# Four fill steps moved from the first expert unit into attention, and one difference moved to GpSimd

## The chip, the cores and the metric

One core of one Trainium2 chip runs the program. The core's engines are TensorE (PE, with its weight loads PEld), VectorE (DVE), ScalarE (ACT), GpSimd (POOL) and SyncE (SP), which issues most DMAs. The metric is the device time of one execution in microseconds.

## The reference

Attention with four sink tokens and a window of 128, then a mixture of eight experts whose gate is normalised by eight Sinkhorn rounds over all tokens:

```python
q, k, v: (4, 8, 768, 64)                      # batch, heads, sequence, head_dim
keep = is_sink | in_window
scores = np.where(keep, scale * q @ k.T, -1e9)
a = softmax(scores);  x = (a @ v) laid out as (3072, 512)

P = np.exp(x @ w_gate - max)                  # (3072, 8)
for _ in range(8):
    P /= P.sum(1, keepdims=True) + 1e-09
    P /= P.sum(0, keepdims=True) + 1e-09
    P *= N / E
for e in range(8):
    out += P[:, e:e + 1] * (np.maximum(x @ w1[e], 0.0) @ w2[e])   # w1: 512x1024, w2: 1024x512
```

## The kernel before

All matrices are kept as a rounded high part and a low part, and a product is three matmuls (high-high, high-low, low-high). The token rows are worked in three parts of 1024.

**Attention.** 48 units, numbered n = 12 b + 2 i + hh over the four sequences b, the six query blocks i of 128 rows and the two halves hh of the heads. The loop `for n in range(-2, L + 3)` runs one round for each: in round n PE does the scores of unit n+1 (L468, into the PSUM banks st0 to st3), the values of unit n-1 (L527), the query and key transposes of unit n+2 (L433), and the transposes of unit n's probabilities (L489, into st1 and st2). Around them VectorE adds the mask (L471), ScalarE exponentiates (L474), GpSimd scales (L478), ScalarE casts the transposed keys and queries (L437) and both split the transposes into PT (L350, cast on ScalarE, subtraction on VectorE). The first block of a sequence (i = 0) has no previous block and no sinks: half the probability transposes and half the value matmuls. PE's order is the program's (`manual_schedule(engines={PE})`); the order on the other engines in this stage is a planner's.

**Fill.** The generator `plain()` computes expert 0 for the first part in 128 steps, numbered 0 to 127: a step is six 128x256 matmuls of a first product (`plain_g1`, L606; two steps make one sum, after which ScalarE does the ReLU, L611, and VectorE its low part, L612), or three 128x512 matmuls of a second product (`plain_g2`, L622). Both kinds alternate, but for the first eight steps (g1 alone) and the last eight (g2 alone). Its weights are split into W1 and W2f by L350; W2f has two buffers. The steps are taken by `run_fill` in the attention rounds from round 5 on, one after the first half of the values and one at the end of the round (92 in all), by the 28 `tick` steps behind attention (REST), and by the eight slots `S_` of the first expert unit (n = 0), which has no earlier unit's second product to put there.

**REST.** In these 28 steps all engines follow the program's order. Step by step they also run the Sinkhorn rounds (`sinkhorn_step`: L48 to L59, with one small matmul, L56, that needs VectorE's csum, L53) and make the x-forms T1, T3 and T2: `make_form` subtracts two raw blocks in two halves (L973), and `form_steps` splits the result (L817 on ScalarE, L818 on VectorE). T1 is made in step 7 and T3 in step 12 on GpSimd, T2 in step 18 on VectorE; `sums1(1)` on GpSimd (L689 to L692) follows in step 23. T2 is split in steps 21 and 22.

**Expert units.** From here each unit of 256 hidden columns runs seven products (M1 to M7, six matmuls each, L791) and the previous unit's second product in the slots `S_`:

```python
STEPS = ["M2", "M1", "M5", S_, "M3", S_, "M6", S_, S_, "M7", S_, S_, "M4", S_, S_]
```

M1, M6, M7 and M4 share PSUM bank c1: each of them waits until VectorE has added the bank's last content into C (L1006, followed by ReLU L1001 and low part L1002). M2, M5 and M3 share c2, copied by ScalarE (L998). The unit's weights W1f come in four pieces, split in unit n for unit n+1 by L817 and L818. Second products (L1035) are added up by VectorE (L630 for fill, L1042 for units).

Parts two and three of the tokens run the same units with stored weights (L791 on W1q, L1350 on W2q).

Of the kernel before, what the change touches and what calls it, by code (L numbers as in the profile page):

```python
# [229 lines left out]
def tile_sink_attention_moe(ctx: ExitStack, tc: tile.TileContext, q, k, v, wg, w1, w2, out):  # L230

    nc = tc.nc
# [75 lines left out]
    def split_gate():  # L308
        for kc in range(KC):
            nc.vector.tensor_copy(wgr[:, kc, :], zero)  # L310
        nc.vector.tensor_copy(wgr[:, :, 0:E], wg_raw)
        nc.vector.tensor_sub(wgr[:, :, E:2 * E], wg_raw, f32(wgr[:, :, 0:E]))
        nc.vector.tensor_add(sel, ident[0:2 * E, 0:E], ident[0:2 * E, E:2 * E])
# [82 lines left out]
    units = [(b, i, hh) for b in range(B) for i in range(NB) for hh in range(2)]  # L396
# [5 lines left out]
    def load_sinks(b):  # L402
        vs = seq[b] = att.tile([SK, D], F32, name="vs")
        for r0 in range(0, SK, NK):
            (nc.sync if b else nc.scalar).dma_start(vs[r0:r0 + NK, :], v[b, :, 0:SINK, :])
# [10 lines left out]
    def load_block(b, i):  # L416
        raws[b, i] = r = [att.tile([P, H, D], F32, name=nm) for nm in ("kr", "qr", "vr")]
        cuts = (0, HH, H) if (b, i) == (0, 0) else (0, H)
        for ts in (((r[0], k), (r[1], q)), ((r[2], v),)):
            for h0, h1 in zip(cuts, cuts[1:]):  # L420
                for t, src in ts:
                    nc.sync.dma_start(t[:, h0:h1, :], src[b, h0:h1, i * P:(i + 1) * P, :].rearrange("h p d -> p h d"))
# [88 lines left out]
    def values(n, pr):  # L511

        b, i, hh = units[n]
        u = us[n]
        if pr == 0:
            u["O"] = ps_o.tile([P, NP, 2, P], F32, name="O")
        cs = slice(pr * P, (pr + 1) * P)
        ops = []
        ws = (1,) if i == 0 else (0, 1)
        for j, w in enumerate(ws):  # L520
            V = us[n - 2 + 2 * w]["V"]
            for x_, y_ in ((0, 0), (0, 1), (1, 0)):
                ops.append((V[:, x_, cs], u["PT", pr][:, y_, j]))
        if i:
            ops.append((seq[b][:, hh * HH * D:][:, cs], u["PS"].unsqueeze(1).broadcast_to([SK, 2, P])))
        for j, (x_, y_) in enumerate(ops):
            nc.tensor.matmul(u["O"][:, pr], lhsT=x_, rhs=y_, start=(j == 0), stop=(j == len(ops) - 1))  # L527
        if pr == NP - 1:
            store_x(n)
# [51 lines left out]
    def gate_step():  # L581
        if gates and next(gates[0], 0) == 0:
            gates.pop(0)
            gate_step()
# [48 lines left out]
    def plain():  # L633

        second = iter(())
        flip = 0
        for us_ in ((0, 1), (2, 3)):
            W = {u: load_plain(0, u) for u in us_}
            for g in range(NG):
                for th in range(2):  # L640
                    hs = []
                    flip = 1 - flip
                    for u in us_:
                        h = hpr.tile([P, 2, HT], F32R, name=f"h{flip}{u % 2}").rearrange("p w (c t) -> p w c t", c=2)
                        for c in range(2):
                            for _ in plain_g1(W, u, c, h, g, th):
                                yield
                                if next(second, 0) is None:
                                    yield
                        hs.append(h)  # L650
                    for _ in second:
                        yield
                    second = plain_g2(W, hs, us_, g, th)
        for _ in second:
            yield

    fill = plain()
# [3 lines left out]
    def run_fill(k_):  # L661
        for _ in range(k_):
            next(fill, None)
# [15 lines left out]
    def blocks(r1):  # L679
        A = r1.rearrange("p (a k) (b f) -> p a b k f", k=KH, b=2)  # L680
        return A[:, 0, 0], A[:, 1, 0], A[:, 0, 1], A[:, 1, 1]

    def sums1(n):

        A11, A12, A21, A22 = blocks(R1[n])
        if n not in ST:
            ST[n] = new_sums()
        S = ST[n]
        nc.gpsimd.tensor_add(S[:, 3], A21, A22)  # L689
        nc.gpsimd.tensor_sub(S[:, 0], S[:, 3], A11)  # L690
        nc.gpsimd.tensor_sub(S[:, 2], A11, A21)
        nc.gpsimd.tensor_sub(S[:, 1], A12, S[:, 0])  # L692
# [25 lines left out]
    with tc.manual_schedule(engines={PE}):  # L718
        for n in range(-2, L + 3):
            on = lambda j: 0 <= j < L  # L720
            if on(n + 2):
                b, i, hh = units[n + 2]
                if hh == 0:
                    with (tc.high_priority() if n == -2 else nullcontext()):
                        load_block(b, i)
                    if i == 0:
                        load_sinks(b)
            if n == -2:
                nc.sync.dma_start(wg_raw, wg.rearrange("(k p) e -> p k e", p=P))
            if n == 2:  # L730
                with tc.issue_after(us[1]["split"][1]):
                    split_gate()
            gates += later
            later.clear()
            if on(n + 1):
                scores(n + 1, 0)
                scores(n + 1, 1)
            if on(n - 1):
                values(n - 1, 0)
            if n >= START:  # L740
                run_fill(1)
            gate_step()
            for j in (0, 1) if n == -2 else (n + 2,) if n >= 0 else ():
                if on(j):
                    transpose_qk(j)
            if on(n):
                transpose_p(n, 0)
                with (tc.issue_after(us[n - 1]["scaled"]) if n > 1 else nullcontext()):
                    split_v(n)
            gate_step()  # L750
            if on(n):
                transpose_p(n, 1)
            if on(n - 1):
                values(n - 1, 1)
            gate_step()
            if on(n) and units[n][1]:
                transpose_sinks(n)
            if on(n) and units[n][1:] == (0, 1):
                with tc.issue_after(us[n]["scaled"]):
                    split_sinks(units[n][0])  # L760
            if n >= START:
                run_fill(1)
            first_w1(n)
        while gates:
            gate_step()
# [203 lines left out]
    def make_form(form, eng=nc.vector):  # L969

        a, b = {"T1": ("B12", "B11"), "T3": ("B22", "B12"), "T2": ("B22", "B11"), "T4": ("B21", "B22")}[form]
        for c in HALVES:
            eng.tensor_sub(raw[PLACE[form]][:, :, c], raw[a][:, :, c], raw[b][:, :, c])  # L973
# [188 lines left out]
    for k in (0, 2, 4, 6, 10, 12, 13, 17, 19, 20, 24, 26, 27):  # L1162
        todo[k].append(sinkhorn_step)
    for k, f in ((7, lambda: make_form("T1", nc.gpsimd)), (12, lambda: make_form("T3", nc.gpsimd)),
                 (18, lambda: make_form("T2")), (23, lambda: sums1(1))):
        todo[k].append(f)
    form_steps(todo, {"T1": (14, 15), "T2": (21, 22), "T3": (24, 25)})
    for k in range(REST):
# [6 lines left out]
    for n in range(len(units0)):  # L1175
        todo = plan(n)
        if n == len(units0) - 1:
            assert not list(side)
            load_x(1, (1, 0), (0, 0), (0, 1), (1, 1))
        run, then, hs[n] = first(n)  # L1180
        sec = second(n - 1, hs[n - 1]) if n else None
        bank = "o" if n else "held1"
        sk_psum = lambda shape, bank=bank: ps0.tile(shape, F32, name=bank, bufs=2 if bank == "o" else 1)
        tight = n == len(units0) - 1
        for k, m in enumerate(STEPS):

            early = m in ("M1", "M6", "M7") and (n < 2 or tight) or m == "M4" and tight
            if early:
                run(m)
                rest = then[m]()  # L1190
                if m == "M4":
                    rest()()
            for f in due.pop(clock[0], ()):
                f()
            for f in todo[k]:
                f()
            if m != S_:
                if not early:
                    run(m)
                    rest = then[m]()  # L1200
                if rest and not (early and m == "M4"):
                    line = due.setdefault(clock[0] + 1, [])
                    line.insert(1 if early else len(line), rest())
            elif n:
                next(sec)()
            else:

                next(fill)
            clock[0] += 1
    assert next(fill, 0) == 0  # L1210
    for k in (16, 17):
# [314 lines left out]
```

## Time and profile before

| what | value |
|---|---|
| median of 3 runs | 2140.49 us (2140.0 to 2141.41) |
| profiled execution | 2140.46 us |
| its span, first to last instruction | 2138.7 us |
| busy: PE, DVE, ACT, POOL | 99%, 72%, 41%, 35% |
| mean granted TensorE clock | 0.997 |
| attention rounds with the changed lines (24, 25, 36, 37) start | 152.8, 158.1, 224.0, 229.2 us |
| REST and the first unit | about 302 to 322.6 us, 322.6 to 338.75 us |

How to read the rows: in the timeline a row has its start in us, its length, the engine, the line, the operation, the tiles out<-in, the shape and the count, and in brackets how long the engine stood idle before it and what ended that. Rows of one kind that follow each other are merged. A window row has the stretch, its length, the busy time of PE, PEld, DVE, ACT and POOL with their counts, the granted clock, the DMA share and GB/s. Matmuls are pipelined and their ends are modelled, so the distance from one row's start to the next is read, not the length.

### The profile page before, as it was taken

How to read it: one execution, taken by the hardware profiler on the slowest of the kernel's cores; microseconds unless marked ns; L12 is line 12 of the kernel's file. 1: busy time of each engine (PE TensorE's matmuls, PEld its weight loads, DVE VectorE, ACT ScalarE, POOL GpSimd, SP SyncE). 2: the span in 40 equal slices, each digit the busy share in tenths (PEclk: the TensorE clock that was granted, in tenths of full speed). 3: DMA queues.
4: the chain of work that ended last, by engine and by line, in shares of the span. 5: the costliest groups of instructions: out<-in, count | busy, mean ns of one | idle time of the engine just before them, and what ended most of it. 6: DMA issues, size and time to landing. Idle time of an engine off the chain costs nothing.

```text
span 2138.7 us, 31819 instructions
## 1 busy us (share of the span) xinstructions
PE 2120.3 (99%) x10501; PEld 1769.8 (83%) x10501; DVE 1538.8 (72%) x2821; ACT 881.9 (41%) x1867; POOL 750.4 (35%) x950
## 2 busy tenths in 40 slices
PE   8999999999999999999999999999999999999998
PEld 7898897888888888888888888888888888888887
DVE  8878868877777776766666666666657666666666
ACT  7777745444444444442333223332333223332322
POOL 7766643233232331232223222233323232233223
PEclk9999999999999999999999999999999999999999
DMA  7434326999999987686666666667866666666662
GB/s 184 95 84 101 86 80 230 314 307 312 294 309 293 310 290 251 216 282 205 204 192 201 208 192 205 203 200 262 297 204 196 199 207 194 200 207 189 205 197 85
DMA packets 397643, 453.83 MB, mean 212 GB/s; under 512 B 99680, under 2 KB 265760, under 8 KB 396576
## 3 DMA queue, kind: packets, MB, share of 16 engines
q1 hardware_dynamic: 397080, 451.57, 68.0%
q8 instruction: 86, 1.41, 0.3%
q14 instruction: 85, 0.70, 0.1%
q10 hardware_dynamic: 392, 0.16, 0.0%
HBM read 314.17 MB, written 137.46 MB: 211 GB/s over the span
## 4 chain that ended last, share of the span: by engine, by line
PE 94%; DVE 3%; ACT 1%; DMA 1%; issue 0%; POOL 0%; SPq 0%; ACTq 0%; DVEq 0%
PE c L791 40%; PE o L1350 20%; PE held L1350 8%; PE held L1035 7%; PE o L1035 7%; PE O L527 3%; PE st L468 2%; PE st L489 1%; PE o L622 1%; PE g L606 1%; ACT sc L474 1%; PE st L433 1%; DVE sc L471 0%; PE O L557 0%; PE st L606 0%
## 5 line engine op out<-in xcount | busy, mean ns | idle before, releaser
L817 ACT CAST hf<-w 128x512 fp32r<-128x512 f32 x448 | 265.0, 620 | 561.5 <-POOL w L1317 299.2
L1350 PE MATMUL o<-hf,W2q 128*128 128x512 f32 x1920 | 472.0, 389 | 0.0
L1350 PEld LDWEIGHTS o<-hf,W2q 128*128 128x128 f32 x1920 | 360.0, 188 | 75.5 <-DVE acc L1364 0.8
L791 PE MATMUL c<-T,W1q 128*128 128x512 f32 x1530 | 389.0, 389 | 0.2 <-DVE w L1298 0.2
L818 DVE TENSOR_TENSOR hf<-w,hf 128x512 fp32r<-128x512 f32 x448 | 330.4, 766 | 74.3 <-ACT hf L817 66.8
L791 PEld LDWEIGHTS c<-T,W1q 128*128 128x128 f32 x1530 | 286.7, 188 | 60.9 <-DVE w L1298 1.2
L1364 DVE TENSOR_TENSOR acc<-o,acc 128x512 f32<-128x512 f32 x298 | 204.6, 687 | 171.5 <-PE o L1350 171.5
L791 PE MATMUL c<-B,W1q 128*128 128x512 f32 x1134 | 278.3, 389 | 0.0
L1317 POOL TENSOR_TENSOR w<-w 128x512 f32<-128x512 f32 x64 | 82.7, 1292 | 493.2 <-DVE w L1299 486.6
L791 PEld LDWEIGHTS c<-B,W1q 128*128 128x128 f32 x1134 | 212.5, 188 | 44.0
L1298 DVE TENSOR_TENSOR w<-c,M 128x512 f32<-128x512 f32 x192 | 132.3, 689 | 138.8 <-PE c L791 133.1
L1294 ACT COPY M<-c 128x512 f32<-128x512 f32 x192 | 112.7, 587 | 250.4 <-PE c L791 250.3
L1350 PE MATMUL held<-hf,W2q 128*128 128x512 f32 x768 | 194.8, 389 | 0.0
L791 PE MATMUL c<-T,W1f 128*128 128x512 f32 x672 | 171.2, 390 | 0.2
L1035 PE MATMUL held<-W2f,h 128*128 128x512 f32 x672 | 171.1, 390 | 0.0
L1035 PE MATMUL o<-W2f,h 128*128 128x512 f32 x672 | 170.6, 389 | 0.1
L1350 PEld LDWEIGHTS held<-hf,W2q 128*128 128x128 f32 x768 | 144.0, 188 | 29.9
L1332 POOL TENSOR_TENSOR w<-w 128x512 f32<-128x512 f32 x64 | 105.7, 1651 | 176.2 <-DVE hf L818 176.2
L1035 PEld LDWEIGHTS o<-W2f,h 128*128 128x128 f32 x672 | 126.0, 188 | 27.0 <-DVE acc L1042 0.9
L791 PEld LDWEIGHTS c<-T,W1f 128*128 128x128 f32 x672 | 125.7, 188 | 27.1 <-ACT M L998 0.5
L1035 PEld LDWEIGHTS held<-W2f,h 128*128 128x128 f32 x672 | 125.8, 188 | 26.4 <-DVE W2f L818 0.5
L844 POOL TENSOR_TENSOR r<-r 128x256 f32<-128x256 f32 x27 | 20.1, 744 | 359.6 <-ACT M L998 210.0
(216 smaller groups left out, 3100.3 us busy)
## 6 DMA issues: line engine op xcount, KB each, us to landing
W2q<-w2s SPq DMA_DIRECT2D x448, 256.0 KB, 3.2
W1q<-w1s SPq DMA_DIRECT2D x444, 256.0 KB, 2.8
w1s<-W1f SPq DMA_DIRECT2D x56, 896.0 KB, 7.6
w2s<-WT SPq DMA_DIRECT2D x136, 256.0 KB, 3.4
r<-in_moe_w_dram SPq DMA_DIRECT2D x64, 512.0 KB, 4.0
w2s<-W2f SPq DMA_DIRECT2D x56, 256.0 KB, 4.8
PB<-psd SPq DMA_DIRECT2D x16, 512.0 KB, 4.2
w2s<-W2f SPq DMA_DIRECT2D x56, 128.0 KB, 6.5
```

Of the source, the lines that this page charges most:

```text
L468: nc.tensor.matmul(ps[h], lhsT=Q[r0:r0 + D, a, pr, :], rhs=K[r0:r0 + D, c, pr, :], start=(j == 0), stop=(j == 2))
L527: nc.tensor.matmul(u["O"][:, pr], lhsT=x_, rhs=y_, start=(j == 0), stop=(j == len(ops) - 1))
L791: nc.tensor.matmul(ps, lhsT=w1(a, k), rhs=x[:, b, k, :], start=(start and j == 0), stop=(stop and j == len(TERMS) - 1), skip_group_check=n ...
L817: nc.scalar.copy(dst[:, 0], src)
L818: at(1, lambda: nc.vector.tensor_sub(dst[:, 1], src, f32(dst[:, 0])))
L1035: nc.tensor.matmul(o, lhsT=h[c, th][:, a, off:off + P], rhs=W2F[n][:, w, c, :], start=(begin and c == 0 and j == 0), stop=(end and c == 1 ...
L1294: nc.scalar.copy(t, T["c2"])
L1298: nc.vector.tensor_add(w, T["c1"], T[m])
L1317: nc.gpsimd.tensor_sub(S3, T["A11"], T["A21"])
L1332: at(k, lambda: nc.gpsimd.tensor_sub(T["A11"], w, T["A11"]))
L1350: nc.tensor.matmul(o, lhsT=W2Q[part, n, m][:, a, k * P:(k + 1) * P], rhs=F[part, n, H_OF[m]][:, w, :], start=(j == 0 and (begin or not hol ...
L1364: nc.vector.tensor_add(sums[m, k], o, sums[m, k])
```

## The change

Three edits. In the rounds of the third and fourth sequences' first blocks (n = 24, 25, 36, 37) the fill call at the end of the round takes two steps instead of one. The fill then has four steps fewer left for the first expert unit: its last four `S_` slots (two behind M7, two behind M4) find none, for which `next` gets a default. And T2's subtraction in REST's step 18 is issued on GpSimd.

```diff
             if n >= START:
-                run_fill(1)
+                run_fill(2 if on(n) and units[n][0] > 1 and units[n][1] == 0 else 1)
             first_w1(n)
...
     for k, f in ((7, lambda: make_form("T1", nc.gpsimd)), (12, lambda: make_form("T3", nc.gpsimd)),
-                 (18, lambda: make_form("T2")), (23, lambda: sums1(1))):
+                 (18, lambda: make_form("T2", nc.gpsimd)), (23, lambda: sums1(1))):
...
-                next(fill)
+                next(fill, None)
```

## Prediction, made before the change was run

> **What bounds the kernel now.** I read the page first, then the stages by windows, then the chain of waits and the timeline of each engine around the four changed rounds and the first expert unit.
>
> ```profile
> span 2138.7 us, 31819 instructions
> PE 2120.3 (99%) x10501; PEld 1769.8 (83%) x10501; DVE 1538.8 (72%) x2821; ACT 881.9 (41%) x1867; POOL 750.4 (35%) x950
> ...
> 302.40:322.60 20.20, 19.83 (x128) 17.51 (x127) 16.24 (x41) 6.42 (x14) 9.19 (x8) 1.00 0.44 155
> ...
> 331.50:338.70 7.20, 7.12 (x31) 5.59 (x32) 6.91 (x15) 3.21 (x7) 0.70 (x2) 1.00 0.01 2
> 338.70:364.60 25.90, 25.52 (x109) 19.25 (x108) 24.96 (x45) 14.25 (x27) 6.25 (x8) 1.00 0.92 299
> ```
>
> TensorE carries nearly the whole span, so the same matmuls in another place change the time only by the waits they fill or leave open. The windows (stretch, its length, then busy time of PE, PEld, DVE, ACT, POOL, then the clock) show two kinds of stage. In the 28 steps between attention and the first unit (302.4 to 322.6) DVE has slack. From the middle of the first unit on (331.5 to 338.7) DVE is busy 6.91 of 7.20 us, and in the second unit 24.96 of 25.90: there PE and DVE are both full. What the change takes out of PE there is worth only what DVE allows.
>
> The chain of waits around rounds 24 to 26 (start, length, what):
>
> ```profile
> 154.84 0.73 PE g L606 x6
> ...
> 157.45 0.71 PE o L622 x3
> 158.16 0.60 PE st L468 x6
> ...
> 159.32 1.88 ACT sc L474 x7
> ...
> 163.76 0.43 DVE sc L471
> ...
> 168.44 1.22 PE st L468 x9
> ```
>
> A fill step of six 128x256 matmuls (L606) holds the chain for 0.73 us, one of three 128x512 (L622) for 0.71. Up to the scores at 158.16 the chain is PE; from there to the scores at 168.44 it runs through ScalarE, GpSimd and VectorE. So a step added at the end of round 24 (before 158.16) moves the chain by its length, and one at the end of round 25 can hide, as far as PE has slack there.
>
> **The change part by part.** *Added steps.* Each pair of changed rounds gets one L606 and one L622 step: 0.73 + 0.71 = 1.44 us of PE, twice. How much of it hides, from the timelines:
>
> ```profile
> 152.81 0.99 PE L468 MATMUL st<-KQ 64*128 64x260 f32 x12
> 153.59 0.43 DVE L471 CUSTOM_DVE_ANT_0 sc<-st,mask 128x260 f32<-128x260 f32 x1 [0.56 <-PE st L468]
> ...
> 162.75 1.24 PE L468 MATMUL st<-KQ 64*128 64x260 f32 x12
> ...
> 166.23 0.36 ACT L611 ACTIVATE h<-g 128x256 fp32r<-128x256 f32 x1
> 166.50 0.57 ACT L437 CAST KQ<-st 128x512 fp32r<-128x512 f32 x1
> ...
> 234.00 1.31 PE L468 MATMUL st<-KQ 64*128 64x260 f32 x12
> ...
> 235.10 0.43 DVE L471 CUSTOM_DVE_ANT_0 sc<-st,mask 128x260 f32<-128x260 f32 x1
> ```
>
> Where DVE waits for the scores, L471 starts 0.78 us after them (152.81 to 153.59). In round 26 PE starts its scores at 162.75 and would now start them at 162.75 + 1.44 = 164.19, so L471 starts at 164.97 where it started at 163.76: 1.21 us later, 0.23 hidden. From there the chain is not PE's. One thing shortens it: the second half of a g1 sum falls to the end of round 25 instead of round 26's first slot, so its ReLU (L611, 0.36) can run while ScalarE waits for scores and no longer stands before the cast L437; that would start 166.50 - 166.23 = 0.27 earlier. Third sequence: +1.21 - 0.27 = +0.94. Fourth sequence, in the same way: 234.00 + 1.44 + 0.78 = 236.22 against 235.10, +1.12; the ReLU of round 38 stays where it is, since that sum's second half still falls to the first slot. Both: +2.06 us. Bounds: +2.88 if nothing hides; and what follows in round 39, where the freed W2f buffer counts:
>
> ```profile
> 239.52 1.15 ACT L350 CAST W2f<-r 128x512 fp32r<-128x512 f32 x2
> ...
> 239.78 1.72 PE L468 MATMUL st<-KQ 64*128 64x260 f32 x11 [0.21 <-DVE PT L350]
> ...
> 240.24 1.56 DVE L350 TENSOR_TENSOR W2f<-r,W2f 128x512 fp32r<-128x512 f32 x2
> ```
>
> These two splits wait for the last fill step that reads the old W2f (step 67 of 0 to 127), which was in round 38 and is now in round 37, and DVE does them ahead of the next L471. Moved into cover they give back 1.56 us; moved into the bare chain of round 38, while the other unit's pair takes their old place in round 39, they cost 1.56 more. The order of these engines is a planner's, and no row shows which; I take 0, and both ends for the range. The casts of W1 move a round in the same manner, with the same two signs.
>
> *T2's difference on GpSimd.*
>
> ```profile
> 309.21 2.75 POOL L973 TENSOR_TENSOR x<-x,x 128x512 f32<-128x512 f32 x2 [0.23 <-DMA x<-xscr]
> 311.92 0.90 POOL L689 TENSOR_TENSOR ST<-r 128x256 f32<-128x256 f32 x1
> ...
> 315.26 1.82 DVE L973 TENSOR_TENSOR x<-x,x 128x512 f32<-128x512 f32 x2
> ...
> 318.22 0.86 PE L622 MATMUL O<-W2f,h 128*128 128x512 f32 x3
> 319.45 0.39 PE L56 MATMUL st<-csum,ones 128*128 128x8 f32 x2 [0.37 <-DVE csum L53]
> ```
>
> DVE loses two subtractions, 1.82 us. GpSimd gains two of about 2.75 / 2 = 1.38 each, right behind T3's (it has no step to wait for), and would be done at 311.96 + 2.75 = 314.7, ahead of DVE's 317.1. Queued behind them on GpSimd stands only the next unit's sums1 (from 311.92), whose product is first used in unit 0's step 13 (W1f's third piece, behind the 337.90 of a row below): covered by over 15 us. DVE is late exactly here: PE waits at 319.45 for csum, which it would otherwise pass at 318.22 + 0.71 = 318.93. That 0.52 us goes. Bounds: 0 and -0.52 (PE has no second wait there). The page "SBUF — State Buffer" of the Trainium skill, section "SBUF: two separate sides", speaks against the move: GpSimd and a DVE instruction with two SBUF inputs lock one another out for the whole instruction. The trace bears this out in one place:
>
> ```profile
> 231.60 1.27 POOL L414 TENSOR_TENSOR VS<-vm,VS 32x512 fp32r<-32x512 f32 x1
> ...
> 231.61 1.28 DVE L475 TENSOR_SCALAR st<-st 128x2 f32<-128x2 f32 x1
> ```
>
> The tiny L475 started with L414 and ended with it. If each T2 half held DVE so, DVE would lose 2 x 1.38 = 2.76 and save 1.82: by the rule the sum is 0.52 to 0.52 + 0.94 worse. I take the gain, because DVE's own T2 already stood beside GpSimd's sums1 and took 1.82.
>
> *Four steps fewer in unit 0.* Its eight slots now hold the steps only up to M6; the two slots behind M7 and the two behind M4 are empty.
>
> ```profile
> 331.46 1.63 PE L622 MATMUL o<-W2f,h 128*128 128x512 f32 x6
> 332.92 1.54 PE L791 MATMUL c<-T,W1f 128*128 128x512 f32 x6
> 334.31 1.52 PE L622 MATMUL o<-W2f,h 128*128 128x512 f32 x6
> 335.13 0.63 DVE L1006 TENSOR_TENSOR C<-c,M 128x512 f32<-128x512 f32 x1
> 335.91 1.63 PE L791 MATMUL c<-T,W1f 128*128 128x512 f32 x6
> 337.37 1.53 PE L622 MATMUL o<-W2f,h 128*128 128x512 f32 x6
> 337.90 1.02 DVE L818 TENSOR_TENSOR W1f<-r,W1f 128x512 fp32r<-128x512 f32 x2
> 338.75 2.88 PE L791 MATMUL c<-B,W1f 128*128 128x512 f32 x12
> ...
> 341.73 0.69 DVE L1006 TENSOR_TENSOR C<-c,M 128x512 f32<-128x512 f32 x1 [0.41 <-PE c L791]
> ```
>
> The fills there took 335.91 - 334.31 = 1.60 and 338.75 - 337.37 = 1.38, 2.98 us in all, of which 0.2 was already waiting. But M4 (335.91) writes bank c1 and must wait for DVE's L1006 (335.13 to 335.76), which stands in DVE's fixed order behind work that does not get shorter; it starts where it does now. And the next unit's M2 (338.75) needs the first W1f piece, whose DVE half runs from 337.90 and takes about 0.69 (two in 1.02, the second half as large): it can start at 338.62. So 2.98 us of PE work turns into waits and only 338.75 - 338.62 = 0.13 comes back. Ends: -0.13 and -2.98. I take -0.13, because DVE's 6.91 of 7.20 us is in the same order before and after; only one accumulate (L630) leaves, behind this point. `next(fill, None)` costs nothing: it issues no instruction.
>
> **Sum:** +2.06 - 0.52 - 0.13 = +1.41 us. The profiled execution took 2140.46 us (its span and 1.8 around it), 0.03 under the median of 2140.49, so both give 2141.9.
>
> **The rivals.** *Unit 0 gives all back* (DVE's order turns out to follow PE): 2141.9 - 2.85 = 2139.0. Against it speaks the 6.91 of 7.20; for it, the 0.41 us that DVE waits for PE at 341.73, right behind.
>
> *The W2f splits fall into cover*: 2141.9 - 1.56 = 2140.3. *They fall before round 38's scores, and the other pair into round 39*: 2143.5. For the second speaks that the buffer gets free in round 37, just ahead of the round with least PE work.
>
> *The lock keeps T2's gain*: 2142.4 to 2143.4.
>
> *Slower: the clock.* Behind M7 and M4 PE would idle some 1.6 and 1.2 us within 6 us. Early in the span the clock fell in such a place:
>
> ```profile
> 16.00:20.00 4.00, 2.74 (x17) 2.38 (x16) 3.81 (x11) 3.87 (x12) 3.82 (x7) 1.00 1.09 361
> ...
> 20.00:28.00 8.00, 6.96 (x41) 6.02 (x42) 7.84 (x28) 5.58 (x17) 5.75 (x15) 0.57 0.46 95
> ...
> 19.62 1.31 PE L468 MATMUL st<-KQ 64*128 64x260 f32 x12 [1.26 <-DVE KQ L438]
> ```
>
> PE was busy 2.74 of 4 us with one wait of 1.26, and over the 8 us behind it the mean granted clock was 0.57. If the same comes here, PE loses 8 x (1 - 0.57) = 3.4 us (an estimate from this row) in a stage without slack: 2145.3. It decides from a loss of 2.9 us on (2144.8). The Trainium skill, "TensorE: Matmul & The Clock Gate", section "Why this matters for your kernels", allows gaps up to about 3 us; by that rule the clock holds and the sum stays as it is. The 1.26 us wait above says that shorter ones can do it.
>
> **How the numbers follow.** Forecast 0.47 (own range 2140.6 to 2143.0), unit 0 gives back 0.10, W2f in cover 0.12, W2f in the chain 0.13, lock 0.08, clock 0.10. No change means within 0.2%, 4.3 us (2136.2 to 2144.8), about what a measurement of this kernel can tell. Slower: half of the clock case and the tail of W2f in the chain, 0.10. Faster needs several gains at once: 0.03. The range 2138.4 to 2145.0 leaves out about half the clock case and some of the first rival's tail.
>
> **What would show it.** Right: rounds 26 and 38 start their scores about 1.2 us later against round 24's and 36's than now; no wait of L56 for csum in the 28 steps; PE idle behind M7 and M4 with L1006 and L818 as releasers; M6 of unit 0 to the next M2 still about 7.2 us. Wrong: that last distance near 4.4 us, a round 39 that is 1.5 us shorter or a longer round 38, or a granted clock under 1.00 behind 330 us.

## The result and the profile after

| | before | after |
|---|---|---|
| median (14 runs each) | 2140.47 us (2139.64 to 2141.41) | 2145.27 us (2144.31 to 2146.41) |
| ratio, with its 95% interval | 1 | 1.0023 (1.0014 to 1.0031) |
| profiled execution | 2140.46 us | 2145.48 us |

The change made the kernel 4.8 us slower; the forecast was +1.4, and 2145.27 lies just above the range, which ended at 2145.0. The page of the kernel after has nearly the same work in a longer span:

```profile
span 2143.7 us, 31817 instructions
PE 2119.1 (99%) x10501; PEld 1769.7 (83%) x10501; DVE 1538.2 (72%) x2819; ACT 882.4 (41%) x1867; POOL 756.1 (35%) x952
```

To see where it went, both spans are cut at the same PE instructions, the first scores (L468) of a round or the first matmul of a product. The table has the length before and the difference after:

| stretch | before, us | after |
|---|---|---|
| start to round 12 | 81.41 | +0.30 |
| rounds 12 to 23 | 71.41 | +0.01 |
| rounds 24 to 35 (third sequence) | 71.15 | -0.08 |
| rounds 36 to 40 (fourth sequence) | 29.87 | **+5.49** |
| rounds 41 to 45, then up to the 28 steps | 48.55 | -0.30 |
| the 28 steps | 20.20 | -0.48 |
| unit 0, M2 to M5 | 2.87 | +1.14 |
| unit 0, M5 to M7 | 7.46 | +0.03 |
| M7 to the next unit's M5 | 8.68 | -0.39 |
| the rest | 1797.14 | -0.78 |

The last row is not the change's work: t2_only and before_late, two of the kernels below, have -0.71 there as well.

The waits of PE between 140 and 380 us (line, releaser, us in total, times, longest) point at the same places:

```profile
PE st L468 <- DVE KQ L438: 4.0, 2, 3.4
PE c L791 <- DVE C L1006: 1.4, 1, 1.4
PE held L56 <- DVE csum L53: 0.9, 1, 0.9
```

The scores' 4.0 us (0.5 before) are in rounds 37 and 38. The timeline of the kernel after there, from several engines (start, length, engine, in brackets the idle time before and its releaser):

```profile
232.50 0.50 ACT L474 ACTIVATE sc<-sc,st 128x260 f32<-128x260 f32 x1
...
233.00 1.12 ACT L350 CAST W2f<-r 128x512 fp32r<-128x512 f32 x2
234.03 0.51 ACT L474 ACTIVATE sc<-sc,st 128x260 f32<-128x260 f32 x1
...
233.63 1.51 DVE L350 TENSOR_TENSOR W2f<-r,W2f 128x512 fp32r<-128x512 f32 x2 [0.31 <-ACT W2f L350]
...
236.28 1.31 PE L468 MATMUL st<-KQ 64*128 64x260 f32 x12 [0.66 <-DVE KQ L438]
...
235.39 0.72 POOL L689 TENSOR_TENSOR r<-r 128x256 f32<-128x256 f32 x1
236.07 0.72 POOL L691 TENSOR_TENSOR r<-r 128x256 f32<-128x256 f32 x1
...
236.82 0.62 ACT L350 CAST W1f<-r 128x512 fp32r<-128x512 f32 x1 [0.92 <-POOL r L691]
...
239.95 0.73 POOL L692 TENSOR_TENSOR r<-r,r 128x256 f32<-128x256 f32 x1
...
240.71 0.62 ACT L350 CAST W1f<-r 128x512 fp32r<-128x512 f32 x1 [3.27 <-POOL r L692]
241.24 0.51 ACT L474 ACTIVATE sc<-sc,st 128x260 f32<-128x260 f32 x1
...
244.84 0.39 PE L468 MATMUL st<-KQ 64*128 64x260 f32 x1 [3.35 <-DVE KQ L438]
245.44 2.12 PE L468 MATMUL st<-KQ 64*128 64x260 f32 x11 [0.21 <-DVE PT L350]
```

Read it from the end. PE waits 3.35 us for KQ (L438), whose cast stands behind round 38's exponentials on ScalarE. These (241.24) could have begun when VectorE's first L471 of that round was done, at 237.8; but in front of them in ScalarE's order stand two casts of W1f, and the second waits 3.27 us for GpSimd's last sum (L692), which GpSimd does between other things. In round 37 (233.00) the two W2f casts split the exponentials, which costs the scores at 236.28 another 0.66.

Behind the long wait the granted clock falls, as the windows show (stretch, length, busy PE, PEld, DVE, ACT, POOL, then the granted clock):

```profile
246.00:248.00 2.00, 1.87 (x9) 1.41 (x9) 1.99 (x3) 0.97 (x3) 1.25 (x2) 0.62 0.00 0
248.00:250.00 2.00, 2.00 (x12) 2.00 (x11) 1.85 (x10) 1.26 (x5) 0.00 (x0) 0.52 0.36 111
250.00:254.00 4.00, 4.00 (x36) 3.59 (x37) 2.85 (x8) 3.04 (x9) 3.42 (x9) 1.00 0.55 125
...
342.00:350.00 8.00, 7.56 (x31) 5.33 (x31) 7.22 (x15) 5.72 (x11) 0.00 (x0) 1.00 0.49 158
```

The granted clock is 0.62 and 0.52 over 4 us, in round 39: by these rows 2 x 0.38 + 2 x 0.48 = 1.7 us of PE (an estimate). So by rounds (scores to scores, after against before): 36 and 37 are 0.70 and 1.35 longer, the two steps' own 1.43 and the 0.62 of the split exponentials; 38 takes 8.56 instead of 5.18; 39 takes 8.92 instead of 8.02, the clock's 1.7 less 0.8 of other work; 40 is 0.84 shorter. Sum: 0.70 + 1.35 + 3.38 + 0.90 - 0.84 = 5.49.

### The profile page after: what moved, and what is told of

It reads as the page before. It is cut to its first block, busy times and chain, and to the rows that moved or that the text cites. A ratio compares the mean times of both kernels' runs of the same rounds, so it can differ in the third digit from the quotient of the medians.

```text
span 2143.7 us, 31817 instructions
## 1 busy us (share of the span) xinstructions
PE 2119.1 (99%) x10501; PEld 1769.7 (83%) x10501; DVE 1538.2 (72%) x2819; ACT 882.4 (41%) x1867; POOL 756.1 (35%) x952
## 4 chain that ended last, share of the span: by engine, by line
PE 94%; DVE 3%; ACT 2%; POOL 1%; issue 0%; DMA 0%; SPq 0%; DVEq 0%; ACTq 0%; POOLq 0%
PE c L791 40%; PE o L1350 20%; PE held L1350 8%; PE held L1035 7%; PE o L1035 7%; PE O L527 3%; PE st L468 2%; PE g L606 2%; PE st L489 2%; PE o L622 1%; ACT sc L474 1%; PE st L433 1%; PE st L606 0%; PE O L622 0%; PE O L557 0%
## 5 line engine op out<-in xcount | busy, mean ns | idle before, releaser
L818 DVE TENSOR_TENSOR hf<-w,hf 128x512 fp32r<-128x512 f32 x448 | 329.1, 763 | 76.0 <-ACT hf L817 68.4
```

The source lines that it names most:

```text
L818: at(1, lambda: nc.vector.tensor_sub(dst[:, 1], src, f32(dst[:, 0])))
```

## Experiments

All kernels were timed against before, medians of 11 runs; before was timed again beside each group and took 2140.36 us (the first four kernels of the table), 2140.32 (the next four) and 2140.28 (the last three). "36-40", "41-45" and so on are differences of one profiled execution to before's, cut as above; parts that are left out (start to round 35, M5 to M7, the rest) scatter too.

| kernel | median, us | ratio (95%) | 36-40 | 41-45 | to 28 steps | 28 steps | M2-M5 | M7 to next M5 |
|---|---|---|---|---|---|---|---|---|
| t2_only | 2140.13 | 0.9999 (0.9990 to 1.0008) | -0.22 | 0 | +0.02 | -0.10 | 0 | 0 |
| fill_only | 2145.53 | 1.0021 (1.0012 to 1.0030) | +7.05 | -0.35 | +0.03 | -0.62 | +0.06 | -0.40 |
| after_hold | 2140.93 | 1.0002 (0.9993 to 1.0012) | +0.91 | +0.59 | +0.47 | -0.56 | +0.09 | -0.41 |
| before_hold | 2140.65 | 1.0001 (0.9992 to 1.0010) | -1.35 | +0.87 | +0.97 | +0.49 | 0 | -0.01 |
| drop4 | 2141.16 | 1.0002 (0.9993 to 1.0012) | +0.01 | -0.02 | +0.02 | +0.01 | 0 | -0.38 |
| seq23 | 2143.06 | 1.0013 (1.0004 to 1.0023) | +2.00 | -0.33 | +0.03 | -0.35 | +0.08 | -0.41 |
| before_late | 2141.72 | 1.0006 (0.9996 to 1.0015) | -2.11 | +3.02 | +0.03 | +0.01 | 0 | +0.01 |
| after_late | 2140.24 | 1.0001 (0.9992 to 1.0010) | -0.55 | +1.43 | +0.01 | -0.54 | +0.08 | -0.38 |
| seq3_rest | 2142.61 | 1.0013 (1.0004 to 1.0022) | +1.52 | +0.25 | +0.37 | +0.67 | -0.01 | -0.41 |
| seq4_rest | 2141.98 | 1.0009 (1.0000 to 1.0018) | +2.14 | +0.21 | +0.39 | +0.67 | -0.01 | -0.40 |
| after_w2late | 2139.78 | 0.9998 (0.9989 to 1.0007) | -0.53 | +0.48 | +0.03 | -0.56 | +0.08 | -0.41 |

**Which part of the change.** t2_only has T2's edit alone, fill_only the rest.

```diff
t2_only:    (18, lambda: make_form("T2", nc.gpsimd))
fill_only:  run_fill(2 if on(n) and units[n][0] > 1 and units[n][1] == 0 else 1)
            next(fill, None)
```

> The kernel before with one edit: T2's two subtractions on GpSimd. Forecast of the prediction: the 0.52 us wait for csum in the 28 steps goes, 2140.0 us. Rival (VectorE and GpSimd hold one another up): in the changed kernel the wait of 0.4 us in the 28 steps is gone but VectorE reaches unit 0 late and the product M5 starts 1.1 us later behind the small Sinkhorn matmul; alone, T2 should then cost 0.3 to 0.9 us, 2140.8 to 2141.4.

> The changed kernel with T2's subtraction back on VectorE, so the moved fill steps alone. If the moved steps are the whole loss, 2145 to 2145.8 us (the forecast's gain of T2 is missing); if T2 on GpSimd costs 0.3 to 0.9 us, 2144.4 to 2145.0. In both cases the rounds 37 to 39 stay as long as in the changed kernel (6.1, 8.6 and 8.9 us).

The fill steps alone give the whole loss. The 7.05 of fill_only beside after's 5.49 is the clock of that one execution, which stayed low for 8 us instead of 4 (lost: 0.70 + 1.00 + 1.00 + 0.72 = 3.4 instead of 1.7):

```profile
246.00:248.00 2.00, 1.88 (x12) 1.27 (x9) 2.00 (x3) 1.19 (x4) 1.48 (x3) 0.65 0.00 0
248.00:250.00 2.00, 2.00 (x10) 2.00 (x10) 1.93 (x10) 1.03 (x5) 0.00 (x0) 0.50 0.24 78
250.00:252.00 2.00, 2.00 (x11) 2.00 (x11) 0.67 (x4) 1.06 (x5) 1.32 (x3) 0.50 0.17 53
252.00:254.00 2.00, 2.00 (x14) 2.00 (x13) 1.10 (x2) 1.26 (x3) 0.56 (x2) 0.64 0.42 96
```

T2 alone is no more than the measurement tells from nothing. Its wait at L56 is gone from the list of PE's waits in t2_only, but the 28 steps became only 0.10 shorter, not 0.52; what took the rest is open.

**Which wait.** after_hold and before_hold hold GpSimd's sums behind the scaling, and the W1f splits behind the splits of PT, of the round in which the program issues them (42 to 45); nothing else is moved. `tc.issue_after` keeps the planner from placing an instruction ahead of the one that it names.

```diff
-            sums1(0)
+            with tc.issue_after(us[n]["scaled"]): sums1(0)
...
-            split(*first_pieces.pop(0))
+            with tc.issue_after(us[n]["split"][0]), tc.issue_after(us[n]["split"][1]): split(*first_pieces.pop(0))
```

> The changed kernel, but the first unit's weight sums and the four casts of its W1f pieces may not be placed ahead of the round that names them (42 to 45). Theory (the planner puts the W1f cast ahead of the exponentials of round 38, where ScalarE waits 3.27 us for GpSimd's sums): round 38 shrinks from 8.6 to about 5.5 us and the time falls by 3 to 4.5 us, to 2140.8 to 2142.3. Rival (the added steps cost their own length and the lost cover in a stage without slack): no change, 2144.8 to 2145.8.

> The kernel before with the same hold on the first unit's weight sums and W1f casts. Theory: round 39, where ScalarE's exponentials stand behind a W1f cast (2.51 us of waiting for GpSimd's sums), shrinks from 8.0 to about 7 us: 0.8 to 1.9 us faster, 2138.6 to 2139.7. Rival: that wait lies beside the W2f splits on VectorE and costs nothing, 2140.5.

The first theory holds: with the sums and W1f casts away, 4.2 of the 4.8 us are back (2140.93 against 2140.36), round 38 takes 5.18 again, and ScalarE in after_hold waits only for VectorE there, although the W2f casts stand where they stood after the change:

```profile
232.97 1.12 ACT L350 CAST W2f<-r 128x512 fp32r<-128x512 f32 x2
...
237.84 0.52 ACT L474 ACTIVATE sc<-sc,st 128x260 f32<-128x260 f32 x1 [1.97 <-DVE st L471]
```

For before_hold a gain was expected, since before has the same pattern one round later; the row is shown below. It did not come: the 1.35 us of rounds 36 to 40 came back, and more, in later rounds, on the way to the 28 steps and in the steps themselves (+0.87, +0.97, +0.49). Held work has to be done later, in rounds with as little room.

**Steps without the fourth sequence, and the gain without the steps.** seq23 puts the four added steps a sequence earlier, into rounds 12, 13, 24 and 25; drop4 adds none and leaves out the last four.

```diff
seq23:  run_fill(2 if on(n) and units[n][0] in (1, 2) and units[n][1] == 0 else 1)   # T2 on VectorE
drop4:  if k < 9:
            next(fill)
```

> The moved fill steps alone (T2 on VectorE), but in the rounds of the second and third sequences' first blocks (12, 13, 24, 25) instead of the third and fourth: no step is added after round 25. Theory (the loss is the early W2f buffer, after which the planner puts the W2f splits, GpSimd's sums and two W1f casts into rounds 37 to 39): the last read of the old W2f is even earlier, in round 36, so these rounds are long again and the time is 2143.5 to 2146. Rival (the loss is that the steps were added in rounds 36 and 37): 2139.9 to 2141.

> The kernel before without the last four fill steps: they are left out altogether (the second product of the last 128 rows of expert 0's second half is missing), so the slots behind M7 and M4 of unit 0 are empty and nothing is added elsewhere. The prediction's step (VectorE's order bounds unit 0): 0.1 to 0.5 us faster, 2139.9 to 2140.3. Rival (unit 0 gives all back): 2.5 to 3 us faster, 2137.4 to 2137.9.

In seq23 rounds 36 and 37 have no added step and rounds 36 to 40 lose 2.00 all the same, this time in round 37 (7.72 for 4.77). That the loss needs the steps there is refuted; the median, 2143.06, is 2.7 us above before's and just under the theory's range, so that the early buffer alone costs the full 5 us is not confirmed. drop4 has unit 0's gain by itself, 0.38 us. Its median is not lower than before's: its profile is 0.62 us later already where the 28 steps begin, with the same code up to there, and has 0.48 more behind the next unit's M5, for which I have no explanation. The interval takes in both no change and the gain.

**The splits held later.** before_late and after_late move both, W2f and W1f, behind chosen rounds.

```diff
+                if u > 1 and j > 1: late.append((d, r)); continue
...
+        if n == L - 8: load1(0)      # in first_w1, whose old lines go
+        with ExitStack() as hold:
+            if n >= START: [hold.enter_context(tc.issue_after(i)) for i in (*us[n]["split"], us[n]["scaled"])] if n < L else None
+            if n in (38, 40): split(*late.pop(0)), split(*late.pop(0))    # before_late: 40, 41
+            if n == L - 7: sums1(0)
+            if n in (L - 6, L - 5): split(*first_pieces.pop(-1 if n == L - 5 else 2))
+        if n == L - 8: first_pieces.extend(pieces1(0)); split(*first_pieces[0]); split(*first_pieces[1])
```

> The kernel before with another placing of the same splits, no fill step moved: the W2f splits of expert 0's second half are held behind rounds 40 and 41 and the sums and two W1f casts behind rounds 41 to 43. Theory (these splits in front of the exponentials make round 39 1.9 and round 40 0.9 us long, and the rounds from 41 on have cover): 1 to 2.5 us faster, 2138 to 2139.4. Rival (as in the run that held W1f alone, what leaves these rounds comes back in later ones): 2140 to 2141.

> The changed kernel with the W2f splits held behind rounds 38 and 40 and the sums and W1f casts behind rounds 41 to 43. Theory: rounds 37 and 38 lose their 1.1 and 3.4 us of extra length, the added steps cost 1 us or less: 2139 to 2141, no slower than the kernel before. Rival (the added steps cost their length): 2142 or more.

after_late takes back all of the loss (2140.24 against 2140.32 for before); before_late gains 2.11 in rounds 36 to 40 and pays 3.02 in the next five. Neither is faster than before.

**What the three share.** seq3_rest and seq4_rest have the added step in one sequence only, and put the other two steps into the 28 steps behind attention; after_w2late holds only the W2f pairs.

```diff
seq3_rest:     run_fill(2 if on(n) and units[n][0] == 2 and units[n][1] == 0 else 1)   # seq4_rest: == 3
               tick(..., (lambda: next(fill)) if k in (20, 24) else None)              # T2 on VectorE in both
after_w2late:  if u > 1 and j > 1: late.append((d, r)); continue
               if n in (38, 40):   # in first_w1
                   with tc.issue_after(us[n]["split"][0]), tc.issue_after(us[n]["split"][1]), tc.issue_after(us[n]["scaled"]): split(*late.pop(0)), split(*late.pop(0))
```

> The change with the added step in the third sequence's rounds only (24, 25); the other two steps are put into two of the 28 steps behind attention (20 and 24), so rounds 36 and 37 have the two steps they had before. Step 67, the last to read the old W2f, falls to the end of round 37, between the change (first slot of round 37) and before (end of round 38). Theory (the earlier buffer lets the W2f and W1f casts and GpSimd's sums stand before round 38's exponentials): rounds 36 to 40 still lose 2 to 5.5 us, median 2142.5 to 2145.5. Rival (the added steps in rounds 36 and 37 are what is late): these rounds take what they took before within 0.3 us, the stage behind attention grows by the 1.4 us of its two steps, unit 0 gives back 0.4, median 2139.5 to 2141.5.

> The mirror of it: the added step in the fourth sequence's rounds only (36, 37), the other two in steps 20 and 24 behind attention. Step 67 falls to the end of round 37 as well. Theory: rounds 36 to 40 lose 2 to 5.5 us, median 2142.5 to 2145.5, and the third sequence's rounds 24 to 35 stay within 0.2 us of before. Rival (added steps late in 36 and 37): the full 5 us of the change here, median about 2145. If both this and its mirror lose nothing, four steps together are needed, which would put it to step 67 in the first slot of round 37 alone.

> The change with only the two late W2f pairs issued later, each held behind the casts and the scaling of its round (38 and 40); GpSimd's sums and the casts of W1f are left where the planner wants them. Theory (the sums and the W1f casts behind them hold up round 38's exponentials, the W2f casts are a small part): rounds 36 to 40 keep at least 3 us of the 5.5 they lost, median 2143 to 2145.5. Rival (the W2f casts are what pushes everything back, as the prediction's case had it): the loss falls to 1 us or less, median 2140 to 2141.2.

seq3_rest decides against the steps' own length: with rounds 36 and 37 nearly as they were (0.00 and +0.12), round 38 takes 8.50 us (after: 8.56). PE waits there in two pieces, and the clock stays at 1.00. The first, 1.40, is for xr (L539), which VectorE does behind the two W2f subtractions (1.57 us from 234.98 on). The second, 1.83, is for KQ, whose cast stands behind the exponentials, and these behind a W1f cast that waits for GpSimd's sums:

```profile
239.07 0.62 ACT L350 CAST W1f<-r 128x512 fp32r<-128x512 f32 x1 [3.60 <-POOL r L691]
...
242.94 0.38 PE L468 MATMUL st<-KQ 64*128 64x260 f32 x1 [1.83 <-DVE KQ L438]
```

Rounds 36 to 40 lose 1.52, less than the 2 that the theory asked for. In seq4_rest they lose 2.14, as expected, but its median, 2141.98, stays under the theory's 2142.5, and its interval begins at no change (1.0000).

after_w2late went against what I expected: the W1f code is untouched, and yet the loss is gone. The reason is a buffer. `sums1(0)` writes into a tile of the same two buffers (`r2` of `rawp`) that hold the raw W2 until the W2f split has read it. So the sums cannot start before that split, whichever kernel one looks at; before, then after_w2late:

```profile
241.88 0.74 POOL L689 TENSOR_TENSOR r<-r 128x256 f32<-128x256 f32 x1 [0.62 <-DVE W2f L350]
...
243.34 0.62 ACT L350 CAST W1f<-r 128x512 fp32r<-128x512 f32 x1 [2.51 <-POOL r L691]
```

```profile
244.75 0.73 POOL L689 TENSOR_TENSOR r<-r 128x256 f32<-128x256 f32 x1 [1.72 <-DVE W2f L350]
```

The same release stands in seq4_rest (237.74) and seq23 (235.47), and in after the sums follow at 235.39, just behind the split's end at 235.14. In after, fill_only and seq3_rest the chain is: fill step 67, W2f split, raw buffer, GpSimd's sums, W1f casts in ScalarE's order, exponentials, keys, scores. Holding it at the W2f split or at the sums frees round 38 of after alike.

In seq4_rest and seq23 the release is early too, but the chain does not run through the W1f casts: these (241.89 and 238.47) wait for nothing. There the two W2f subtractions themselves stand on VectorE ahead of L471, and ScalarE's exponentials wait for L471, in round 38 of seq4_rest and in round 37 of seq23:

```profile
235.95 1.71 DVE L350 TENSOR_TENSOR W2f<-r,W2f 128x512 fp32r<-128x512 f32 x2
...
238.04 0.51 ACT L474 ACTIVATE sc<-sc,st 128x260 f32<-128x260 f32 x1 [1.60 <-DVE st L471]
```

```profile
231.96 3.37 DVE L350 TENSOR_TENSOR W2f<-r,W2f 128x512 fp32r<-128x512 f32 x2
...
235.71 0.52 ACT L474 ACTIVATE sc<-sc,st 128x260 f32<-128x260 f32 x1 [3.02 <-DVE st L471]
```

This is the prediction's own case, the splits in the bare chain. So an earlier step 67 costs in two ways, and how much depends on what meets where it falls: 1.5 to 2.1 us in three kernels, 5.5 and 7.1 in the two with all four steps where the change has them. Of these the low clock is, by the windows, about 1.7 in after and in seq4_rest, 3.4 in fill_only and nothing in seq3_rest and seq23.

## Why the prediction was wrong

*The step that failed* is "The order of these engines is a planner's, and no row shows which; I take 0", with ends of 1.56 us. The row quoted there was VectorE's two W2f splits, and their 1.56 became the price. That is what the splits take, not what they release. GpSimd's sums and the W1f casts that wait for them are not in the working at all; all that it says of further casts is "The casts of W1 move a round in the same manner, with the same two signs", and W1 is the fill's own weight. They were most of the cost: round 38 became 3.38 us longer, and holding them alone (after_hold) gave this back. Before's own trace had the row that prices it, the W1f cast with 2.51 us of idle ScalarE ahead of it (243.34 above), in the same round 39 as the W2f pair. The case "in the chain" (2143.5) was the right sort and too small: the fourth sequence was forecast at +1.12, or +2.68 in that case, and measured +5.49, of which some 1.7 is the clock's.

*Third sequence, +0.94:* measured -0.08. As far as the forecast goes it held: against round 24's scores, L471 of round 26 came 1.18 later (forecast 1.21) and the cast L437 0.92 (forecast 0.94). But it stopped there and took what was left as lost. Rounds 24 and 25 are longer by 0.70 and 0.72, and rounds 26 to 29 give back 0.27, 0.23, 0.15 and 0.80. In round 29 of before a split of the fill's W1 stands on VectorE (179.29) ahead of the keys; in after it stands elsewhere, which may be what gave the 0.80. No run tests this.

*Scores of rounds 26 and 38 about 1.2 us later:* they came 1.43 and 2.05 later. By the prediction's own working the scores had to move by 1.44 and only L471 by 1.21, so the sign named the wrong row. In round 38 the 0.62 of the split exponentials is on top.

*T2, -0.52:* the wait at L56 did go, in t2_only and in after. Alone the edit is worth 0.1 in the 28 steps. In after the steps gained 0.48, but fill_only has 0.62 there with T2 still on VectorE, so that gain belongs to the shifted steps. And only in after, in its one profiled execution, a wait for csum stands in unit 0's M5, in the rows below: two L818 of VectorE take 2.39 us beside GpSimd's next form (L973). Singly they take 0.68 and 1.78; the second starts 0.05 us behind L973.

```profile
326.94 2.39 DVE L818 TENSOR_TENSOR T<-x,T 128x512 fp32r<-128x512 f32 x2
...
327.49 2.99 POOL L973 TENSOR_TENSOR B<-B,x 128x512 f32<-128x512 f32 x2 [3.91 <-PE O L622]
...
331.29 0.39 PE L56 MATMUL held<-csum,ones 128*128 128x8 f32 x2 [0.88 <-DVE csum L53]
...
337.56 1.63 PE L622 MATMUL o<-W2f,h 128*128 128x512 f32 x6
339.03 1.54 PE L791 MATMUL c<-T,W1f 128*128 128x512 f32 x6
342.01 1.63 PE L791 MATMUL c<-T,W1f 128*128 128x512 f32 x6 [1.44 <-DVE C L1006]
343.48 1.08 PE L791 MATMUL c<-B,W1f 128*128 128x512 f32 x4
344.75 0.73 PE L791 MATMUL c<-B,W1f 128*128 128x512 f32 x2 [0.19 <-DVE W1f L818]
```

The same two in after_late, with the same code in this stage, begin 0.79 us ahead of L973 (in after 0.55), take 1.29, and M5 has no wait. The second starts 0.20 us ahead of L973 there:

```profile
321.99 1.29 DVE L818 TENSOR_TENSOR T<-x,T 128x512 fp32r<-128x512 f32 x2
...
322.78 3.01 POOL L973 TENSOR_TENSOR B<-B,x 128x512 f32<-128x512 f32 x2 [4.14 <-PE O L622]
```

So the hold-up that the rival named is there, by about 1.1 us, on work next to T2's rather than on T2. By the Trainium skill, "SBUF — State Buffer", section "SBUF: two separate sides", the operation that starts first keeps the other out for its whole length. These rows agree: the second L818 fell on the wrong side of a start in after, and on the right one in after_late. The tiny L475, which the prediction set beside that rule, reads one tile only, so these rows are the closer case. The medians do not show the 1.1 us: the loss is 4.8 us with T2's edit and 5.2 without it (2145.53 against 2140.36).

*Unit 0, -0.13* (by its own rows, 337.90 + 0.69, rather -0.16): measured -0.38 to -0.41 in every kernel with the steps moved, and in drop4. M4 waits for L1006 (342.01) as forecast. What was missed: the next M2 (343.48) needs ScalarE's high part of W1f for its first four matmuls and VectorE's low part only for the last two, which wait at 344.75. From the slots behind M6 to it are 343.48 - 337.56 = 5.92 us, where before had 338.75 - 331.46 = 7.29 and the forecast wanted that kept. But M2 and M1 then take 3.84 us up to M5 (347.32) instead of 2.86, broken up by two short waits of 0.19 and 0.20, so that only 0.39 stays. "Unit 0 gives all back" is refuted.

*The clock.* Behind 330 us it held (1.00 in 342 to 350, behind a wait of 1.44), as the forecast had it. The mechanism that I named as a rival came in another place, behind the wait of 3.35 us at 244.84, and cost about 1.7 us there. The Trainium skill, "TensorE: Matmul & The Clock Gate", section "Why this matters for your kernels", warns of idle gaps over some 3 us; 3.35 agrees. In seq4_rest the clock fell behind shorter ones too, as the last section shows.

## What to carry to other kernels

When a step moves, price not only the step and the split that waits for it, but everything that the freed buffer lets start, down to the last user in a fixed order; look in the trace of before for an in-order engine that already stood idle ahead of such a cast. A cast whose input is another engine's late result, placed ahead of an exponential, can hand that engine's lateness on to everything behind it (here 3.27 us on ScalarE and 3.35 on PE), and a fall of the clock may follow. Holding the release back undoes such a loss, but held work needs room later: none of these kernels beat the one before.

## What the runs showed of the hardware

*The clock falls behind waits of very different length.* In seq4_rest PE waited 0.51, 0.79 and 0.21 us within 5 us, and about 2 us behind the last of them the granted clock was 0.51 and 0.64 for two stretches of 2 us:

```profile
241.54 0.39 PE L468 MATMUL st<-KQ 64*128 64x260 f32 x1 [0.79 <-DVE KQ L438]
```

```profile
244.00:246.00 2.00, 2.00 (x13) 2.00 (x12) 2.00 (x9) 1.84 (x9) 0.12 (x1) 0.51 0.44 131
246.00:248.00 2.00, 2.00 (x14) 2.00 (x14) 0.88 (x5) 1.04 (x3) 1.79 (x4) 0.64 0.02 6
```

That is, by these rows, 2 x 0.49 + 2 x 0.36 = 1.7 of its 2.14 us. In seq23 a wait of 2.14 us, with 0.65 and 0.42 behind it (238.56 and 244.19), left it at 1.00:

```profile
235.82 0.41 PE L489 MATMUL st<-ident,sc 128*128 128x128 f32 x2 [2.14 <-DVE st L471]
```

```profile
234.00:238.00 4.00, 2.08 (x14) 1.63 (x14) 3.71 (x12) 2.29 (x9) 3.23 (x5) 1.00 0.62 135
238.00:250.00 12.00, 10.80 (x89) 9.52 (x90) 11.05 (x38) 9.88 (x32) 9.73 (x21) 1.00 0.20 50
```

So the length of the longest wait does not decide it; what does is open. These are single profiled executions. The same goes for the start: over the first 30 us the mean clock was 0.89 in before, 0.97 in after and 0.81 in after_w2late, and the time up to round 12 was -0.30 to +1.36 us against before's, in kernels whose code is the same there. The clock alone does not explain it: after, with 0.97, was 0.30 us later, and seq4_rest, with 0.83, 0.19 earlier.

*VectorE behind GpSimd.* In four places a VectorE subtraction of two SBUF tiles ends 0.54 to 0.55 us behind the GpSimd subtraction beside it: the second L818 of after (L973's first half ends at 328.78), the first W2f subtraction of seq4_rest (L448 ends at 236.49), and both W2f subtractions of seq23 (L448 and L414 end at 233.11 and 234.78), which take 1.70 and 1.74 us. In after_late the pair takes 1.29 us together, so by that measure some 2.1 of the 3.37 us in seq23 are this hold-up and not work (an estimate).
